# A GEGLU feed-forward kernel: first loads in a forced order, zero matmuls at the start, transposes of x by DMA, and halves outside quarters

## The chip, the cores and the metric

One core of one Trainium2 chip. The metric is device time in microseconds (us) of the whole program. The span is the time from the first to the last instruction in the profiled run; it is 1.7 to 2.0 us shorter than the time of that run.

## The reference

```python
B, S, D, F = 1, 2048, 1024, 3584          # bf16
def reference(x, w_gate, w_up, w_down):
    return (_gelu(x @ w_gate) * (x @ w_up)) @ w_down
```

## The kernel before

x is worked in two blocks of 1024 rows, each in two halves of 512 (`sh`). A block has a first phase (g = gate matmuls, u = up matmuls, then GELU on ACT and a product on DVE into hT) and a second phase (o = down matmuls). The weights of the first phase come in seven groups (`fg`) of 1 MB each for gate and up; each group has four quarters (`fi`) of 128 columns. The matmuls need x transposed. The tensor engine (PE) does that, in chunks (`sc`) of 128 rows, and DVE copies each chunk out of PSUM.

```python
w_pool = ...tile_pool(name="wstream", bufs=3)
xnat_pool = ...tile_pool(name="xnat", bufs=3)      # room for three x chunks
def load_xT_chunk(blk, sc):
    x_nat = xnat_pool.tile([P, D], bf16, name="x_nat")
    nc.sync.dma_start(out=x_nat[:], in_=x2[row0:row0 + P, :])
    for dc in range(DC):
        nc.tensor.transpose(pT[:, dc, :], x_nat[:, dc * P:(dc + 1) * P], ident[:])
    nc.vector.tensor_copy(out=xT_t[:, :, off:off + P], in_=pT[:])

for sc in range(SCB):                               # eight chunks first
    load_xT_chunk(0, sc)
for blk in range(NBLK):
    for fg in range(NFG):
        # 1 MB of gate, 1 MB of up, in block 0 also 1 MB of down, all on nc.sync
        for fi in range(FG):
            for sh in range(NSH):                   # quarter outer, half inner
                # 8 g matmuls, 8 u matmuls, gelu (ACT), product (DVE) -> hT
    for sc in range(SCB):
        # 2 x 28 o matmuls, copies (ACT), store (nc.scalar)
        if blk + 1 < NBLK:
            load_xT_chunk(blk + 1, sc)              # next block's x, on PE
```

## Time and profile before

| | before |
|---|---|
| time, median of 4 runs | 608.31 us (606.58 to 608.51) |
| span of the profiled run | 606.7 us |
| PE busy | 98%, 2816 matmuls and transposes |
| DVE, ACT busy | 14%, 14% |
| DMA | 74 GB/s of HBM traffic over the span |

PE is busy nearly throughout, so its busy share cannot tell where time is to be had. The readings that can are the chain that ended last, which names what the end of the program waited for, step by step, and the timeline of the first 25 us.

### The profile page before, as it was taken

The page shows a single profiled execution, that of the slowest core. Times are in us where ns is not written, and L with a number is a line of the kernel's source. Part 1 is how long each engine was busy: PE and PEld are TensorE (multiplying, and loading weights), DVE is VectorE, ACT ScalarE, POOL GpSimd, SP SyncE. Part 2 cuts the span into 40 slices and gives each one's busy share as a digit, 9 for nine tenths or more (in the row PEclk, how much of TensorE's full clock was granted, in tenths as well). Part 3 has the DMA queues.
Part 4 walks back from the last instruction along what each step waited for, and adds up shares of the span by engine and source line. Part 5 has one row for each costly group of instructions (what it writes and reads, how often), then busy time and mean ns, then how long its engine had stood idle before and what let it go on. Part 6 is the DMA issues. An engine that isn't in the chain of part 4 may idle for free.

```text
span 606.7 us, 6223 instructions
## 1 busy us (share of the span) xinstructions
PE 591.7 (98%) x2816; PEld 272.2 (45%) x2816; DVE 87.9 (14%) x128; ACT 86.9 (14%) x145; POOL 0.7 (0%) x6
## 2 busy tenths in 40 slices
PE   3999999999999999999999999999999999999997
PEld 2444444444444444444444444444444444444443
DVE  1221211212112100000001212112121120000000
ACT  0111111111111100101011111111111111101010
POOL 0000000000000000000000000000000000000000
PEclk9999999999999999999999999999999999999999
DMA  8997032140404041011000404041300000000000
GB/s 295 351 323 260 24 115 90 50 138 1 139 0 139 0 156 54 35 36 35 36 18 0 139 0 139 0 140 34 106 1 0 1 0 1 17 36 17 18 18 35
DMA packets 37451, 45.49 MB, mean 75 GB/s; under 512 B 1072, under 2 KB 29744, under 8 KB 37424
## 3 DMA queue, kind: packets, MB, share of 16 engines
q1 hardware_dynamic: 35120, 40.90, 20.8%
q10 hardware_dynamic: 2304, 4.20, 1.8%
q8 instruction: 22, 0.36, 0.2%
q14 instruction: 5, 0.04, 0.0%
HBM read 40.89 MB, written 4.19 MB: 74 GB/s over the span
## 4 chain that ended last, share of the span: by engine, by line
PE 97%; DMA 2%; DVE 0%; issue 0%; ACT 0%
PE g_ps L109 32%; PE u_ps L114 32%; PE o_ps L131 32%; DMA x_nat<-in_x_dram 2%; PE pT L79 1%; DVE xT L81 0%; DVE hT L120 0%; ACT o_sb L136 0%
## 5 line engine op out<-in xcount | busy, mean ns | idle before, releaser
L109 PE MATMUL g_ps<-xT,wg 128*128 128x512 bf16 x896 | 212.9, 381 | 0.6 <-DVE xT L81 0.6
L114 PE MATMUL u_ps<-xT,wu 128*128 128x512 bf16 x896 | 211.8, 379 | 0.0
L131 PE MATMUL o_ps<-wd,hT 128*128 128x512 bf16 x896 | 195.0, 379 | 0.0
L109 PEld LDWEIGHTS <-wg 128*128 128x128 bf16 x896 | 88.0, 98 | 107.0 <-issue 2.5
L114 PEld LDWEIGHTS <-wu 128*128 128x128 bf16 x896 | 87.7, 98 | 105.6
L131 PEld LDWEIGHTS <-hT 128*128 128x128 bf16 x896 | 87.3, 98 | 104.0 <-DVE hT L120 0.2
L120 DVE TENSOR_TENSOR hT<-hT,u_ps 128x512 bf16<-128x512 bf16 x112 | 77.1, 688 | 308.0 <-PE u_ps L114 308.0
L119 ACT ACTIVATE hT<-g_ps 128x512 bf16<-128x512 f32 x112 | 66.9, 597 | 335.2 <-PE g_ps L109 335.2
L136 ACT CAST o_sb<-o_ps 128x512 bf16<-128x512 f32 x32 | 18.8, 586 | 180.7 <-PE o_ps L131 180.7
L81 DVE COPY xT<-pT 128x1024 bf16<-128x1024 bf16 x16 | 11.0, 691 | 111.2 <-PE pT L79 111.2
L79 PE MATMUL pT<-ident,x_nat 128*128 128x128 bf16 x128 | 11.5, 248 | 10.7 <-DMA x_nat<-in_x_dram 10.6
L79 PEld LDWEIGHTS <-x_nat 128*128 128x128 bf16 x128 | 9.8, 112 | 13.6 <-DMA x_nat<-in_x_dram 11.1
L119 ACT ACT_TABLE_LOAD x1 | 1.3, 1283 | 0.7 <-PEq L154 0.7
masks.py:199 POOL TENSOR_SCALAR_AFFINE_SELECT ident<-ident 128x128 bf16<-128x128 bf16 x1 | 0.3, 294 | 0.1
masks.py:197 POOL MEMSET ident<- 128x128 bf16 x1 | 0.2, 205 | 0.3 <-POOLq L154 0.3
L154 POOL MEMSET const-uint8-127<- 128x1 uint8 x1 | 0.1, 103 | 0.0
L154 POOL MEMSET const-bfloat16-1.0<- 128x1 bf16 x1 | 0.1, 102 | 0.0
L154 POOL MEMSET const-float32-0.0<- 128x1 f32 x1 | 0.1, 99 | 0.2 <-issue 0.2
L154 POOL MEMSET const-float32-1.0<- 128x1 f32 x1 | 0.1, 99 | 0.0
## 6 DMA issues: line engine op xcount, KB each, us to landing
wg<-in_w_gate_dram SPq DMA_DIRECT2D x14, 1024.0 KB, 5.2
wu<-in_w_up_dram SPq DMA_DIRECT2D x14, 1024.0 KB, 7.7
wd<-in_w_down_dram SPq DMA_DIRECT2D x7, 1024.0 KB, 12.3
x_nat<-in_x_dram SPq DMA_DIRECT2D x16, 256.0 KB, 3.4
out_dram<-o_sb ACTq DMA_DIRECT2D x16, 256.0 KB, 2.0
```

What stands on the lines that cost most here:

```text
L79: nc.tensor.transpose(pT[:, dc, :], x_nat[:, dc * P:(dc + 1) * P], ident[:])
L81: nc.vector.tensor_copy(out=xT_t[:, :, off:off + P], in_=pT[:])
L109: nc.tensor.matmul(g_ps[:], lhsT=wg_t[:, dc, fi * P:(fi + 1) * P], rhs=xT_t[:, dc, :], start=(dc == 0), stop=(dc == DC - 1),)
L114: nc.tensor.matmul(u_ps[:], lhsT=wu_t[:, dc, fi * P:(fi + 1) * P], rhs=xT_t[:, dc, :], start=(dc == 0), stop=(dc == DC - 1),)
L119: nc.scalar.activation(h_t[:], g_ps[:], ACT.Gelu_apprx_tanh)
L120: nc.vector.tensor_tensor(out=h_t[:], in0=h_t[:], in1=u_ps[:], op=ALU.mult)
L131: nc.tensor.matmul(o_ps[:], lhsT=hT[(fc, sh)][:, off:off + P], rhs=wd_tiles[fc // FG][:, fc % FG, dh * DH:(dh + 1) * DH], start=(fc == 0), ...
L136: nc.scalar.copy(out=o_sb[:, dh * DH:(dh + 1) * DH], in_=o_ps[:])
L154: nc = _bacc.Bacc("TRN2", target_bir_lowering=False, num_devices=1)
```

## The change

It is meant to shorten everything that is not one of the 2688 large matmuls. It sends the first half of x and the first weights off at once on two hardware queues, in a forced order. It runs eight matmuls of zeros while PE would wait. It transposes only the first half of x on PE and leaves the other three halves to DMA transposes. It reads the first weight group in quarters, so that the first one is there early, and puts the halves outside the quarters in every group, so that the second half of x is wanted later. The order on PE is fixed by hand. Besides, the down weights are loaded one group later, the streamed weights have two buffers rather than three, and the output tiles share eight buffers with x. The cut below is shortened; `...` marks what is left out.

```diff
+N_WARM = 8; IO_BUFS = 8; W_BUFS = 2; FORCE_DMA_ORDER = True
-    w_pool = ...(name="wstream", bufs=3); xnat_pool = ...bufs=3; o_pool = ...bufs=2
+    w_pool = ...(name="wstream", bufs=W_BUFS); io_pool = ...(name="io", bufs=IO_BUFS)
+    zt = const_pool.tile([P, WN], bf16, name="zt")
+    nc.vector.memset(zt[:], 0.0)
+    for i in range(N_WARM):
+        nc.tensor.matmul(warm_ps[:, :WN], lhsT=zt[:, 0:P], rhs=zt[:, :], start=True, stop=True)
+    ctx.enter_context(tc.manual_schedule(engines={mybir.EngineType.PE}))
+    def load_xT_half_dma(blk, sh, dma_eng):
+        dma_eng.dma_start_transpose(out=xT_t[:, :, :], in_=x2[row0:row0 + SH, :])
-    for sc in range(SCB):
-        load_xT_chunk(0, sc)
+    for sc in range(SCH):      # x chunks 0, 2 on sync, 1, 3 on scalar
+        load_x_nat(0, sc, nc.sync if sc % 2 == 0 else nc.scalar, ...)
+    for fi in range(FG):       # quarters: rows of 256 B
+        stamp(nc.sync.dma_start(out=wg0_t[:, :, fi * P:(fi + 1) * P], ...), "sp")
+        stamp(nc.scalar.dma_start(out=wu0_t[:, :, fi * P:(fi + 1) * P], ...), "act")
+    for sh in range(1, NSH):
+        load_xT_half_dma(0, sh, nc.sync)
+    for sc in range(SCH):
+        transpose_x_chunk(0, sc)
 ...
+            # block 0, from fg 2 on: one DMA transpose of a half of block 1 per group
-            for fi in range(FG):
-                for sh in range(NSH):
+            for sh in range(NSH):
+                for fi in range(FG):
+                    phase1_group(blk, fg * FG + fi, sh, wg_t, wu_t, fi, hT)
 ...
-            if blk + 1 < NBLK:
-                load_xT_chunk(blk + 1, sc)
```

More of the change, by code (lines that the diff above doesn't have):

```diff
@@ L10 @@
 ALU = mybir.AluOpType
+N_WARM = 8
+IO_BUFS = 8
+W_BUFS = 2
+FORCE_DMA_ORDER = True
 @with_exitstack
@@ L54 @@
     hT_pool = ctx.enter_context(tc.tile_pool(name="hT", bufs=FC * NSH))
-    w_pool = ctx.enter_context(tc.tile_pool(name="wstream", bufs=3))
-    xnat_pool = ctx.enter_context(tc.tile_pool(name="xnat", bufs=3))
-    o_pool = ctx.enter_context(tc.tile_pool(name="osb", bufs=2))
+    w_pool = ctx.enter_context(tc.tile_pool(name="wstream", bufs=W_BUFS))
+    io_pool = ctx.enter_context(tc.tile_pool(name="io", bufs=IO_BUFS))
     ps_g = ctx.enter_context(tc.tile_pool(name="ps_g", bufs=2, space=bass.MemoryType.PSUM))
@@ L61, with stamp, get_xT @@
     ps_t = ctx.enter_context(tc.tile_pool(name="ps_t", bufs=2, space=bass.MemoryType.PSUM))
+    if N_WARM > 0:
+        WN = min(SH, DH)
+        zt = const_pool.tile([P, WN], bf16, name="zt")
+        nc.vector.memset(zt[:], 0.0)
+        warm_ps = ps_o.tile([P, DH], f32, name="o_ps")
+        for i in range(N_WARM):
+            nc.tensor.matmul(warm_ps[:, :WN], lhsT=zt[:, 0:P], rhs=zt[:, :], start=True, stop=True)
     ident = const_pool.tile([P, P], bf16, name="ident")
     make_identity(nc, ident[:])
+    def stamp(inst, tok):
+        if FORCE_DMA_ORDER and tok is not None:
+            tc.stamp_issue_order_token(inst.ins, tok)
+    ctx.enter_context(tc.manual_schedule(engines={mybir.EngineType.PE}))
     xT_tiles = {}
-    def load_xT_chunk(blk, sc):
-        sh = sc // SCH
+    def get_xT(blk, sh):
         key = (blk, sh)
@@ L72, in load_xT_chunk, with load_x_nat, transpose_x_chunk @@
             xT_tiles[key] = xT_pool.tile([P, DC, SH], bf16, name="xT")
-        xT_t = xT_tiles[key]
+        return xT_tiles[key]
+    x_nat_tiles = {}
+    def load_x_nat(blk, sc, dma_eng, tok=None):
         row0 = blk * SBLK + sc * P
-        x_nat = xnat_pool.tile([P, D], bf16, name="x_nat")
-        nc.sync.dma_start(out=x_nat[:], in_=x2[row0:row0 + P, :])
+        x_nat = io_pool.tile([P, D], bf16, name="io")
+        stamp(dma_eng.dma_start(out=x_nat[:], in_=x2[row0:row0 + P, :]), tok)
+        x_nat_tiles[(blk, sc)] = x_nat
+    def transpose_x_chunk(blk, sc):
+        sh = sc // SCH
+        xT_t = get_xT(blk, sh)
+        x_nat = x_nat_tiles.pop((blk, sc))
         pT = ps_t.tile([P, DC, P], bf16, name="pT")
@@ L81, in load_xT_chunk, with load_wd, phase1_group @@
         nc.vector.tensor_copy(out=xT_t[:, :, off:off + P], in_=pT[:])
+    def load_xT_half_dma(blk, sh, dma_eng):
+        xT_t = get_xT(blk, sh)
+        row0 = blk * SBLK + sh * SH
+        dma_eng.dma_start_transpose(out=xT_t[:, :, :], in_=x2[row0:row0 + SH, :])
     wd_tiles = []
-    def load_wd(fg):
+    def load_wd(fg, dma_eng):
         t = wd_pool.tile([P, FG, D], bf16, name="wd")
-        nc.sync.dma_start(out=t[:], in_=wd_v[:, fg * FG:(fg + 1) * FG, :])
+        dma_eng.dma_start(out=t[:], in_=wd_v[:, fg * FG:(fg + 1) * FG, :])
         wd_tiles.append(t)
-    for sc in range(SCB):
-        load_xT_chunk(0, sc)
+    def phase1_group(blk, fc, sh, wg_t, wu_t, fi, hT):
+        xT_t = xT_tiles[(blk, sh)]
+        g_ps = ps_g.tile([P, SH], f32, name="g_ps")
+        u_ps = ps_u.tile([P, SH], f32, name="u_ps")
+        for dc in range(DC):
+            nc.tensor.matmul(
+                g_ps[:], lhsT=wg_t[:, dc, fi * P:(fi + 1) * P], rhs=xT_t[:, dc, :],
+                start=(dc == 0), stop=(dc == DC - 1),
+            )
+        for dc in range(DC):
+            nc.tensor.matmul(
+                u_ps[:], lhsT=wu_t[:, dc, fi * P:(fi + 1) * P], rhs=xT_t[:, dc, :],
+                start=(dc == 0), stop=(dc == DC - 1),
+            )
+        h_t = hT_pool.tile([P, SH], bf16, name="hT")
+        nc.scalar.activation(h_t[:], g_ps[:], ACT.Gelu_apprx_tanh)
+        nc.vector.tensor_tensor(out=h_t[:], in0=h_t[:], in1=u_ps[:], op=ALU.mult)
+        hT[(fc, sh)] = h_t
+    wg0_t = w_pool.tile([P, DC, FG * P], bf16, name="wg")
+    wu0_t = w_pool.tile([P, DC, FG * P], bf16, name="wu")
+    for sc in range(SCH):
+        load_x_nat(0, sc, nc.sync if sc % 2 == 0 else nc.scalar, "sp" if sc % 2 == 0 else "act")
+    for fi in range(FG):
+        stamp(nc.sync.dma_start(out=wg0_t[:, :, fi * P:(fi + 1) * P],
+                                in_=wg_v[:, :, fi * P:(fi + 1) * P]), "sp")
+        stamp(nc.scalar.dma_start(out=wu0_t[:, :, fi * P:(fi + 1) * P],
+                                  in_=wu_v[:, :, fi * P:(fi + 1) * P]), "act")
+    for sh in range(1, NSH):
+        load_xT_half_dma(0, sh, nc.sync)
+    for sc in range(SCH):
+        transpose_x_chunk(0, sc)
+    pending_xT = [(b_, sh_) for b_ in range(1, NBLK) for sh_ in range(NSH)]
     for blk in range(NBLK):
@@ L95 @@
         for fg in range(NFG):
-            wg_t = w_pool.tile([P, DC, FG * P], bf16, name="wg")
-            nc.sync.dma_start(out=wg_t[:], in_=wg_v[:, :, fg * FG * P:(fg + 1) * FG * P])
-            wu_t = w_pool.tile([P, DC, FG * P], bf16, name="wu")
-            nc.sync.dma_start(out=wu_t[:], in_=wu_v[:, :, fg * FG * P:(fg + 1) * FG * P])
-            if blk == 0:
-                load_wd(fg)
-            for fi in range(FG):
-                fc = fg * FG + fi
-                for sh in range(NSH):
-                    xT_t = xT_tiles[(blk, sh)]
-                    g_ps = ps_g.tile([P, SH], f32, name="g_ps")
-                    u_ps = ps_u.tile([P, SH], f32, name="u_ps")
-                    for dc in range(DC):
-                        nc.tensor.matmul(
-                            g_ps[:], lhsT=wg_t[:, dc, fi * P:(fi + 1) * P], rhs=xT_t[:, dc, :],
-                            start=(dc == 0), stop=(dc == DC - 1),
-                        )
-                    for dc in range(DC):
-                        nc.tensor.matmul(
-                            u_ps[:], lhsT=wu_t[:, dc, fi * P:(fi + 1) * P], rhs=xT_t[:, dc, :],
-                            start=(dc == 0), stop=(dc == DC - 1),
-                        )
-                    h_t = hT_pool.tile([P, SH], bf16, name="hT")
-                    nc.scalar.activation(h_t[:], g_ps[:], ACT.Gelu_apprx_tanh)
-                    nc.vector.tensor_tensor(out=h_t[:], in0=h_t[:], in1=u_ps[:], op=ALU.mult)
-                    hT[(fc, sh)] = h_t
@@ new lines @@
+            c0 = fg * FG * P
+            if blk == 0 and fg == 0:
+                wg_t, wu_t = wg0_t, wu0_t
+            else:
+                wg_t = w_pool.tile([P, DC, FG * P], bf16, name="wg")
+                wu_t = w_pool.tile([P, DC, FG * P], bf16, name="wu")
+                nc.sync.dma_start(out=wg_t[:], in_=wg_v[:, :, c0:c0 + FG * P])
+                nc.sync.dma_start(out=wu_t[:], in_=wu_v[:, :, c0:c0 + FG * P])
+            if blk == 0:
+                if fg >= 1:
+                    load_wd(fg - 1, nc.sync)
+                if fg == NFG - 1:
+                    load_wd(fg, nc.sync)
@@ L123 @@
+            if blk == 0 and pending_xT and (fg >= 2 or fg == NFG - 1):
+                n_issue = 1 if fg < NFG - 1 else len(pending_xT)
+                for _ in range(n_issue):
+                    b_, sh_ = pending_xT.pop(0)
+                    load_xT_half_dma(b_, sh_, nc.sync)
+            for sh in range(NSH):
+                for fi in range(FG):
+                    phase1_group(blk, fg * FG + fi, sh, wg_t, wu_t, fi, hT)
         for sc in range(SCB):
@@ L126 @@
             row0 = blk * SBLK + sc * P
-            o_sb = o_pool.tile([P, D], bf16, name="o_sb")
+            o_sb = io_pool.tile([P, D], bf16, name="io")
             for dh in range(NDH):
```

## The prediction

> **What bounds the kernel now.** I read the page's busy shares first, then the chain that ended last, because busy time of pipelined matmuls does not say how close to its floor the engine runs.
>
> ```profile
> span 606.7 us, 6223 instructions
> PE 591.7 (98%) x2816; PEld 272.2 (45%) x2816; DVE 87.9 (14%) x128; ACT 86.9 (14%) x145; POOL 0.7 (0%) x6
> PE g_ps L109 32%; PE u_ps L114 32%; PE o_ps L131 32%; DMA x_nat<-in_x_dram 2%; PE pT L79 1%; DVE xT L81 0%; DVE hT L120 0%; ACT o_sb L136 0%
> L79 PE MATMUL pT<-ident,x_nat 128*128 128x128 bf16 x128 | 11.5, 248 | 10.7 <-DMA x_nat<-in_x_dram 10.6
> ```
>
> The tensor engine is the chain: 96% is the three matmul groups, 2% waiting for x, 1% transposes of x. DVE and ACT are 14% busy and release nothing late. So only the 2%, the 1% and the pace of the matmuls are to be had. The chain in order of time gives the pace and the head (columns: start, length, what):
>
> ```profile
> 0.74 2.56 DMA x_nat<-in_x_dram
> 4.41 9.02 DMA x_nat<-in_x_dram
> 13.47 1.89 PE pT L79 x16
> 15.36 3.06 PE g_ps L109 x8
> 22.96 1.89 PE g_ps L109 x8
> 506.27 96.71 PE o_ps L131 x448
> ```
>
> The last row is the pace: 96.71 / 448 = 0.2159 us for each 128x512 matmul. There are 3 x 896 = 2688, so the unavoidable part is 580.3 us. The span is 606.7, so 26.4 us are something else. The timeline tells what (start, length, engine, line, what):
>
> ```profile
> 19.77 0.61 PE L79 MATMUL pT<-ident,x_nat 128*128 128x128 bf16 x8
> 20.43 1.33 PE L79 MATMUL pT<-ident,x_nat 128*128 128x128 bf16 x16
> 22.96 1.89 PE L109 MATMUL g_ps<-xT,wg 128*128 128x512 bf16 x8 [0.59 <-DVE xT L81]
> 224.54 0.61 PE L79 MATMUL pT<-ident,x_nat 128*128 128x128 bf16 x8
> 603.00 0.59 ACT L136 CAST o_sb<-o_ps 128x512 bf16<-128x512 f32 x1 [5.46 <-PE o_ps L131]
> ```
>
> The account of the 26.4 us:
> - 15.4 us until the first g matmul at 15.36. The fourth x chunk has a buffer only at 4.41 and then queues behind 2 MB of gate and up weights, hence the 9.02 us in the chain.
> - 1.3 us: the first eight g matmuls take 3.06 us, where eight at pace take 1.73.
> - 2.4 us: from 18.42 to 22.96 (4.54 us) the engine does eight u and, reordered forward, two o matmuls, ten at pace = 2.16 us; the rest, 2.4, is transposes of the second half of x and a wait on their copy.
> - 3.5 us: eight chunks of the next block are transposed between o groups. A pair of o groups with its transposes repeats every 12.53 us; 56 matmuls at pace are 12.09; 8 x 0.44 = 3.5.
> - 3.7 us after the last matmul (602.98 to 606.7): last copy and last store.
> They sum to 26.3, so nothing large is hidden elsewhere.
>
> **What the Trainium skill says.** (1) "TensorE: Matmul & The Clock Gate", Part 1: the array starts at half clock, is released after about 3.4 us of sustained activity, and falls back after an idle window of about that length; warm matmuls of 512 columns follow each other at N/2.4 + 2.5 ns, 215.8. The trace agrees: 215.9 ns, and a slow first eight. (2) "DMA: Bandwidth & Descriptors", Specifications: transfers want rows of at least 512 B, below it there is a read-modify-write. The trace has only rows of 1 and 2 KB in bulk (364 to 376 GB/s between 7 and 12 us in the windows view), so what 256 B rows do is not shown. (3) The same page, Latency and other measured facts: a crossbar DMA transpose moved 261 GB/s in one kernel. (4) "VectorE: DVE Perf Modes", The three transpose paths: one 128x128 block by that path takes 1309 ns. No run here shows either yet, and they are far apart: 1 MB at 261 GB/s is 4.0 us, 32 blocks end to end would be 42 us.
>
> **The change part by part.**
>
> *Early loads.* Four x chunks go out at once, two on each hardware queue, ahead of any weight, with four buffers of their own. In the windows view the core had moved 0.83 MB by 5 us and 1.1 MB by 6:
>
> ```profile
> 2.00:3.00 1.00, 0.00 (x0) 0.00 (x0) 0.00 (x0) 0.02 (x1) 0.00 (x0) 1.00 1.01 318
> 3.00:4.00 1.00, 0.65 (x7) 0.66 (x8) 0.00 (x0) 0.00 (x0) 0.00 (x0) 1.00 0.73 225
> 10.00:11.00 1.00, 0.00 (x0) 0.00 (x0) 0.00 (x0) 0.00 (x0) 0.00 (x0) 1.00 1.08 368
> ```
>
> (last column GB/s, the one before it the share of the DMA engines; the dip at 3 to 5 us is beside slow issue on one queue). With two queues I put the 1 MB of x at about 5.2 us. Then the first quarter of gate and up, 0.52 MB in 256 B rows: I take half of 368 GB/s as an estimate from point (2), 2.9 us, plus 0.5 for landing: 8.6. The transposes of the fourth chunk (0.95 us) and its copy (0.69) fit before that. First g matmul at about 9.0 instead of 15.36: 6.4 us gained.
>
> *Warm-up.* Eight zero matmuls of 512 columns at half clock, 8 x 0.43 = 3.4 us, stand in front of the transposes and fit in the wait for x, which in the trace ends at 3.3. They cost about nothing and should let the first g group run at pace: 1.3 us gained.
>
> *Second half of x and all of the second block by DMA transpose.* Of 128 PE transposes 96 go, and 12 copies on DVE. On the path: the 2.4 us around 20 us and the 3.5 us between the o groups: 5.9 us gained.
>
> *Order and buffers.* Manual order of the tensor engine ends the pulling forward of o matmuls; nothing else in it moves. With two weight buffers rather than three, a load may start when the group before last is done, and has one group's time, 8 x 8 x 2 x 0.2159 = 27.6 us, to arrive; the page has 5.2 and 7.7 us to landing. Hidden. The tail is untouched.
>
> *Supply.* This is the new cost. With the halves outer, the first 4 groups read only the first half of x, but all four quarters of gate and up: one pair per 3.45 us, at 2.9 us supply. The pairs come just ahead. The last pair has left the queue at 5.2 + 4 x 2.9 = 16.8; then the transpose of the second half, behind them on the same queue: 4.0 us at 261 GB/s plus some 1.5 for landing, 22.3. It is wanted at 9.0 + 4 x 3.45 = 22.8. There is no slack, so any slower rate than either assumption is paid in full: at half the transpose rate 4 us. I book 2.0 us.
>
> Sum: -6.4 - 1.3 - 5.9 + 2.0 = -11.6; 608.3 - 11.6 = 596.7; I say 596.5. As a cross-check: 9.0 + 580.3 + 3.7 = 593.0 of span, and runs are 1.6 us longer than the profiled span (608.31 against 606.7): 594.6 with no stall.
>
> **The rivals.**
>
> *The transpose DMA takes the place of the wait removed.* If the crossbar moves about 75 GB/s, the second half lands near 32 us, the engine idles 9 us at the end of the first four groups, goes cold, and the time is 604 to 606. For it: the figure of 1309 ns a block, and no trace of this path. Against: someone laid out one such transfer per later weight group, where it is hidden anyway, and put only one at the critical place. The second block's transfers have over 150 us; they cannot matter.
>
> *Narrow rows starve the start.* If 256 B rows cost as much time as 1 KB rows (47 ns per packet and engine: 16 x 1.08 x 1024 B / 368 GB/s), a pair takes 6 us, the four pairs end at 29, and everything after is late by 8 to 13 us: 603 to 608, no gain. For it: the pace per packet in the trace is only known where bytes bind. Against: 1 KB and 2 KB rows move at nearly equal rates, so a fixed cost per row is not seen at 1 KB.
>
> *All fits.* Both assumptions are a little pessimistic, t0 is 8.5 and no stall: 594. For it: queues issue at 0.4 us each and two share the start.
>
> **Range and chances.** The gain without stalls is 13.6 us, 2.2%, so the 2% line (596.1) leaves only 1.5 us for stalls. Stalls under 1.5 us I hold for 0.46, between that and 26 us for 0.51, above 26 for 0.03, which would need the transpose DMA to take 30 us. The range 592.5 to 604.0 leaves out the full form of the first two rivals.
>
> **What would show it.** Right: first g matmul near 9 us and its eight taking 1.7 to 1.9 us; 32 PE transposes; no transposes among the o groups, which then run at 0.2159 without a break; last matmul to end still 3.7 us. Wrong: gaps before g or u groups put down to the weight DMAs (narrow rows), or one gap before the fifth pair put down to xT by DMA (slow transpose); or a wait for weights in later groups (two buffers too few).

## The result, and the profile after

| | before | after |
|---|---|---|
| median | 608.23 us (13 runs, 606.58 to 608.54) | 594.08 us (8 runs, 593.78 to 596.69) |
| span of the profiled run | 606.7 us | 592.2 us |
| first g matmul starts | 15.36 us | 8.35 us |
| PE transposes | 128 | 32 |

The ratio is 0.9777, with a 95% interval of 0.9765 to 0.9789: faster by 2.2%. Ratios are the mean time of one kernel's runs over that of the other's of the same rounds, so they are not quite the ratio of the medians quoted. The predicted time was 596.5 with a range of 592.5 to 604.0. The measured time lies in the range, 2.4 us below the point. Of the three chances, "within 2%" had 0.51 and "faster by over 2%" 0.46; the second came, so the class held for slightly more likely did not.

The page of the changed kernel, busy shares and chain by line:

```profile
PE 586.4 (99%) x2728; PEld 266.4 (45%) x2728; DVE 79.9 (13%) x117; ACT 87.0 (15%) x145; POOL 0.7 (0%) x6
PE g_ps L126 33%; PE o_ps L189 33%; PE u_ps L131 33%; PE o_ps L73 1%; DVE xT L107 0%; PE pT L105 0%; ACT io L194 0%; DVE zt L70 0%
```

No DMA is left in the chain: before, x had 2% of it. What remains is 33% for each kind of matmul and 1% for the zero matmuls (L73). Rows of the timeline of PE, its weight loads (PEld), DVE and SyncE's queue (SPq) in the first 25 us (start, length, engine, line, what, idle before and what ended it):

```profile
1.19 3.59 PE L73 MATMUL o_ps<-zt 128*128 128x512 bf16 x8 [1.19 <-DVE zt L70]
4.57 1.45 PE L105 MATMUL pT<-ident,io 128*128 128x128 bf16 x16
5.62 2.68 DVE L107 COPY xT<-pT 128x1024 bf16<-128x1024 bf16 x4 [4.49 <-PE pT L105]
7.82 9.06 SPq L112 DMA_TRANSPOSE xT<-in_x_dram  x1
7.84 0.10 PEld L126 LDWEIGHTS <-wg 128*128 128x128 bf16 x1 [0.45 <-DMA wg<-in_w_gate_dram]
8.35 1.89 PE L126 MATMUL g_ps<-xT,wg 128*128 128x512 bf16 x8 [0.78 <-DVE xT L107]
...
22.16 1.89 PE L126 MATMUL g_ps<-xT,wg 128*128 128x512 bf16 x8
```

The g row at 8.35 is the new start. The first gate quarter has landed at 7.84 and what is waited for last is the fourth copy on DVE, from a row of four that ends at 8.30. The next u group begins 1.72 us later, which is eight times the pace of 0.2159: no slow first group. The g row at 22.16 is the first that reads the second half of x, and it has no wait in brackets. By the view of the DMA transpose's source, that transfer took 12.7 us from its issue at 7.82, so it landed at 20.5, 1.7 us before it was wanted. Most of that time it stood behind the weight quarters. From 16 to 18 us the queue moved nothing but its rows of 256 B, at 290 GB/s (columns: us, busy time by engine, granted clock, DMA share, GB/s):

```profile
16.00:18.00 2.00, 2.00 (x11) 0.88 (x9) 0.21 (x1) 0.60 (x1) 0.00 (x0) 1.00 1.28 290
```

From 8.35 to the end of the last matmul nothing stops PE: in the changed trace the second phase of the first block takes from 201.73 to 298.43, 96.70 us for 448 matmuls, where the kernel before had 8 x 12.53 = 100.2. The chain in order of time has them as one piece (start, length, what):

```profile
201.90 96.69 PE o_ps L189 x448
```

So the 14.5 us between the two spans are:

| where | before | after | gain |
|---|---|---|---|
| start of the first g group | 15.36 | 8.35 | 7.0 |
| first g group, over the pace | 1.3 | 0 | 1.3 |
| transposes and their wait near 20 us | 2.4 | 0 | 2.4 |
| transposes among the o groups | 3.5 | 0 | 3.5 |
| after the last matmul | 3.7 | 3.5 | 0.2 |

They add up to 14.4.

### The profile page after: what moved, and what is told of

It reads as the page before. It is cut to its first block, busy times and chain, and to the rows that moved or that the text cites. A ratio compares the mean times of both kernels' runs of the same rounds, so it can differ in the third digit from the quotient of the medians.

```text
span 592.2 us, 6019 instructions
## 1 busy us (share of the span) xinstructions
PE 586.4 (99%) x2728; PEld 266.4 (45%) x2728; DVE 79.9 (13%) x117; ACT 87.0 (15%) x145; POOL 0.7 (0%) x6
## 4 chain that ended last, share of the span: by engine, by line
PE 99%; DVE 0%; ACT 0%; issue 0%
PE g_ps L126 33%; PE o_ps L189 33%; PE u_ps L131 33%; PE o_ps L73 1%; DVE xT L107 0%; PE pT L105 0%; ACT io L194 0%; DVE zt L70 0%
## 5 line engine op out<-in xcount | busy, mean ns | idle before, releaser
L194 ACT CAST io<-o_ps 128x512 bf16<-128x512 f32 x32 | 18.8, 586 | 178.1 <-PE o_ps L189 178.1
L73 PE MATMUL o_ps<-zt 128*128 128x512 bf16 x8 | 3.6, 631 | 1.2 <-DVE zt L70 1.2
L107 DVE COPY xT<-pT 128x1024 bf16<-128x1024 bf16 x4 | 2.6, 686 | 4.6 <-PE pT L105 4.5
L105 PE MATMUL pT<-ident,io 128*128 128x128 bf16 x32 | 2.7, 241 | 0.3 <-DVE xT L107 0.3
L105 PEld LDWEIGHTS <-io 128*128 128x128 bf16 x32 | 2.4, 110 | 1.2 <-issue 0.6
L73 PEld LDWEIGHTS <-zt 128*128 128x128 bf16 x8 | 1.0, 140 | 2.8 <-issue 1.7
```

The lines of the kernel that those rows point to most:

```text
L73: nc.tensor.matmul(warm_ps[:, :WN], lhsT=zt[:, 0:P], rhs=zt[:, :], start=True, stop=True)
L194: nc.scalar.copy(out=o_sb[:, dh * DH:(dh + 1) * DH], in_=o_ps[:])
```

## The experiments

My theory after the result: five places add up, and what makes the gain come in full is that two new supplies (weight quarters, DMA transpose) are both just in time. Its rivals: one part alone (x earlier, or the forced order) makes the gain and the rest is idle; or the zero matmuls do nothing; or the DMA transpose is in time under any order. Each edit below is to the changed kernel unless said otherwise. The extra time of an edit is given against the change's median of 594.08 or its span of 592.2. The experiments ran in later rounds on chips 14, 6 and 1; the kernel before ran beside them, with medians of 608.23, 608.39 and 607.93 us, so differences of a few tenths of a us are not read.

### nowarm, nowarm2, nowarm3: without the zero matmuls

```diff
-N_WARM = 8
+N_WARM = 0
```

> The change without its eight zero matmuls. My theory: the array is still at half clock when the first g group starts, so that group takes about 3.1 us rather than 1.9 as in the kernel before; against that the transposes can begin some 0.4 us earlier, since in the changed kernel they wait for the zero matmuls as long as for x. Net: 1.0 us longer than the change, about 595.1. Rival: the 32 transposes warm the array themselves; then the first g group takes 1.9 us and the run is equal to the change or 0.4 us faster.

Measured: 595.1 us in the median of four runs, but these are two pairs: 593.99 and 594.18, 596.03 and 596.41. The traced one was a quick one, with a first g group at pace at 8.58. So the median met the theory while the trace met the rival.

> The kernel without zero matmuls once more, for its trace alone: its runs fell into 594.0 to 594.2 and 596.0 to 596.4, and only a quick one was traced, in which the first g group ran at pace. My theory now: the slow ones are those in which the array is still at half clock in the first g groups (1.7 us each); if this look is a slow one, its first g group takes over 3 us and starts near 8.6 as well. Rival: the slow ones wait for data, so the first g group starts 2 us later and takes 1.9.

> The same kernel a third time, to have a second chance of a slow run in the trace; the expectations are those of the look before it.

The first of these looks took 594.18 us, the second 596.67: a quick and a slow one. First PE's timeline in nowarm2, the quick one:

```profile
4.09 3.68 PE L105 MATMUL pT<-ident,io 128*128 128x128 bf16 x32 [4.09 <-DMA io<-in_x_dram]
8.56 1.89 PE L126 MATMUL g_ps<-xT,wg 128*128 128x512 bf16 x8 [0.78 <-DVE xT L107]
```

Then in nowarm3, the slow one:

```profile
4.46 3.68 PE L105 MATMUL pT<-ident,io 128*128 128x128 bf16 x32 [4.46 <-DMA io<-in_x_dram]
8.93 3.57 PE L126 MATMUL g_ps<-xT,wg 128*128 128x512 bf16 x8 [0.78 <-DVE xT L107]
12.29 2.39 PE L131 MATMUL u_ps<-xT,wu 128*128 128x512 bf16 x8
```

The slow run starts 0.4 us later, and its first g and u group take 3.36 us and 2.23 us to the start of the next rather than 1.73: 2.1 us over the pace together. With the 0.4 that is the 2.5 us between the two spans (594.9 and 592.4). So without the zero matmuls the array can still be at half clock when the first group starts. That is shown in one slow run; the two other slow ones of six (596.03 and 596.41) were not traced, and that they have the same cause is likely and not shown. With the zero matmuls, one of the change's eight runs (596.69) is slow. In the quick runs that were traced the 32 transposes alone had warmed the array. Both theory and rival held, in different runs. What the zero matmuls are worth in the mean is not settled: the means differ by 0.8 us, but the ratios to the kernel before, 0.9781 (0.9761 to 0.9802) and 0.9777 for the change, do not tell them apart, and the recorded verdict is unclear. They mostly take away spread.

### fiouter: quarter outer, half inner, as before

```diff
-            for sh in range(NSH):
-                for fi in range(FG):
+            for fi in range(FG):
+                for sh in range(NSH):
```

> The change with the old loop order, quarter outer and half inner. My theory: the halves-outer order is what hides the DMA transpose. The second half of x lands at 20.5 us in the changed kernel and is wanted at 11.8 us here, so the tensor engine stalls 8.7 us once, goes cold for another 1.3 us, and the run is about 604. Rival: the order only helps the weights, and the transpose would be in time anyway: 594.

Measured: 602.92 us (602.59 to 603.17), 8.8 over the change. PE's timeline in fiouter:

```profile
9.88 1.89 PE L131 MATMUL u_ps<-xT,wu 128*128 128x512 bf16 x7
18.84 3.47 PE L126 MATMUL g_ps<-xT,wg 128*128 128x512 bf16 x8 [7.07 <-DMA xT<-in_x_dram]
22.14 1.89 PE L131 MATMUL u_ps<-xT,wu 128*128 128x512 bf16 x8
```

One stall of 7.07 us, ended by the DMA transpose, and behind it a g group at half clock (3.30 us from 18.84 to 22.14). The transfer landed at 18.8 here and not at 20.5, which is why the stall is shorter than expected. The order of the loops is what hides the transpose: swapped back, most of the gain is gone.

### wide: first weights in rows of 1 KB

```diff
-    for fi in range(FG):
-        ... dma_start(out=wg0_t[:, :, fi * P:(fi + 1) * P], ...)   # and wu0_t
+    ... dma_start(out=wg0_t[:], in_=wg_v[:, :, 0:FG * P])          # and wu0_t
```

> The change with the first gate and up weights in one transfer each with rows of 1 KB, not four quarters with rows of 256 B. My theory: the first g group now has to wait for all of gate, which shares the engines with up; 1 MB of x and 2 MB of weights at about 350 GB/s land near 11.5 us, so the first g matmul comes about 3 us later than 8.35 and the run is about 597. Rival: the narrow rows (218 GB/s in the changed trace) lose what the quarters gain, and the run is within 0.5 us of the change.

Measured: 600.99 us (600.1 to 601.28), 6.9 over the change; the profiled run has 5.9 more span. PE's timeline in wide:

```profile
11.35 3.60 PE L126 MATMUL g_ps<-xT,wg 128*128 128x512 bf16 x8 [3.48 <-DMA wg<-in_w_gate_dram]
...
17.59 1.89 PE L126 MATMUL g_ps<-xT,wg 128*128 128x512 bf16 x8
```

The start is at 11.35, 3.0 later, as the theory said. What it left out is the clock: PE idled 3.48 us, and the next 16 matmuls took 6.24 us (17.59 - 11.35) instead of 3.45. 3.0 + 2.8 are the 5.9, within rounding. So the narrow rows pay although they are slow. The windows view of the changed kernel has them by themselves at 9 to 10 us (last columns: granted clock, DMA share, GB/s):

```profile
9.00:10.00 1.00, 1.00 (x6) 0.48 (x5) 0.00 (x0) 1.00 (x1) 0.00 (x0) 1.00 1.35 218
```

218 GB/s against 364 to 376 for rows of 1 KB in the kernel before: 0.59 of it.

### blk1pe: second block of x on PE again

```diff
-                    load_xT_half_dma(b_, sh_, nc.sync)      # block 1, with its loop
+            if blk + 1 < NBLK:                              # after each output tile
+                load_x_nat(blk + 1, sc, nc.sync)
+                transpose_x_chunk(blk + 1, sc)
```

> The change with the second block of x transposed on the tensor engine between the o groups again, as in the kernel before. My theory: 64 transposes cost 8 x 0.44 = 3.5 us of the engine, and nothing else moves: 597.6. Rival: the DMA transposes cost something too (disturbed weight loads), so that undoing them costs less than 3.5 us.

Measured: 597.62 us (597.49 to 598.06), 3.5 over the change, the number of the theory. PE's timeline in blk1pe:

```profile
202.04 12.25 PE L183 MATMUL o_ps<-wd,hT 128*128 128x512 bf16 x55
214.13 0.61 PE L105 MATMUL pT<-ident,io 128*128 128x128 bf16 x8
214.57 12.25 PE L183 MATMUL o_ps<-wd,hT 128*128 128x512 bf16 x54
```

A row of transposes stands between o groups that start at 202.04 and 214.57: 12.53 us, as in the kernel before.

### half1pe: second half of the first block on PE

```diff
-        load_xT_half_dma(0, sh, nc.sync)
+        load_x_nat(0, sc, nc.sync)                          # four chunks
+                if blk == 0 and fg == 0 and sh == 1:
+                    for sc in range(SCH, SCB):
+                        transpose_x_chunk(0, sc)
```

> The change with the second half of the first block loaded plainly and transposed on the tensor engine between its first four and next four groups, in place of the DMA transpose. My theory: the engine pays 32 transposes (1.8 us) and waits for the four copies behind them (4 x 0.69, the first starting 0.5 us in): 3.3 us between 22.2 and 25.5, so 597.4. Rival: the DMA transpose is worth no more than its 1.8 us of matmuls, because the copies overlap: 595.9.

Measured: 598.21 us (598.05 to 598.74), 4.1 over the change. PE's timeline in half1pe:

```profile
22.22 1.06 PE L105 MATMUL pT<-ident,io 128*128 128x128 bf16 x16
23.83 1.21 PE L105 MATMUL pT<-ident,io 128*128 128x128 bf16 x16 [0.55 <-DVE xT L107]
25.82 1.90 PE L126 MATMUL g_ps<-xT,wg 128*128 128x512 bf16 x8 [0.79 <-DVE xT L107]
```

From 22.22 to 25.82 are 3.6 us: the transposes and two waits on DVE's copies (0.55 and 0.79 of them visible in the brackets). The theory had 3.3, the rival 1.8. The profiled run also has half a microsecond more after the last matmul, which I do not explain. The DMA transpose of this half is worth more than the transposes themselves, because PE does not wait for copies.

### noorder: first transfers in the scheduler's own order

```diff
-FORCE_DMA_ORDER = True
+FORCE_DMA_ORDER = False
```

> The change without the forced order of its first transfers. The built program then has x chunk, gate quarter, x chunk, gate quarters on one queue, and up quarter, x chunk, up quarter, x chunk, up quarters on the other. My theory: the last x chunk lands behind up to 1 MB of narrow rows, near 9 us rather than 5.5 to 6; transposes and copy put the first g matmul near 10.6 rather than 8.35: 2.2 us, and up to 1.5 more if the array goes cold meanwhile: 596.3 to 597.8. Rival: the same bytes have to come anyway, so the first g group waits no longer: 594.

Measured: 600.17 us (599.05 to 600.52), 6.1 over the change and outside both expectations. PE's timeline in noorder:

```profile
10.16 1.04 PE L105 MATMUL pT<-ident,io 128*128 128x128 bf16 x8 [1.44 <-DMA io<-in_x_dram]
11.98 3.57 PE L126 MATMUL g_ps<-xT,wg 128*128 128x512 bf16 x8 [0.78 <-DVE xT L107]
...
18.24 1.89 PE L126 MATMUL g_ps<-xT,wg 128*128 128x512 bf16 x8
```

The last x chunk landed at 10.1 rather than near 9, the first g group came at 11.98, 3.6 later than in the change, and its 16 matmuls with u ran cold: 18.24 - 11.98 = 6.26 us, 2.8 over the pace. The mechanism was right, the size short by the second cold group and one more microsecond of landing.

### earlyx: the kernel before with five x buffers

```diff
-    xnat_pool = ...tile_pool(name="xnat", bufs=3)
+    xnat_pool = ...tile_pool(name="xnat", bufs=5)
```

> The kernel before with one number changed: five buffers for x chunks rather than three, so that the first half of x is not queued behind the weights. My theory: this alone takes back most of the head. Gate lands near 9 us and the first g matmul comes then instead of at 15.4; but the last three chunks still land behind up, near 13.5 us, and their transposes stand in the middle of the first g group, so that group ends near 15 us. From there 2680 matmuls at 0.2159, 3.5 us of later transposes and 3.7 of tail: a span near 601 and a time near 602.5, 6 us under the kernel before. Rival: it is the order of the weights that sets the start, and x earlier only moves the wait: within 1 us of 608.

Measured: 605.85 us (605.18 to 606.65) against 608.39 of the kernel before in the same rounds, ratio 0.9961 (0.9947 to 0.9975): 2.5 us, not 6. PE's timeline in earlyx:

```profile
10.34 1.25 PE L109 MATMUL g_ps<-xT,wg 128*128 128x512 bf16 x5 [1.65 <-DMA wg<-in_w_gate_dram]
14.00 1.03 PE L79 MATMUL pT<-ident,x_nat 128*128 128x128 bf16 x8 [2.41 <-DMA x_nat<-in_x_dram]
...
20.01 1.89 PE L109 MATMUL g_ps<-xT,wg 128*128 128x512 bf16 x8
```

The first g matmul is indeed 5 us earlier. But gate lands at 10.3 and not 9, the group is broken off for the last three chunks, which land behind up, and its last matmuls and the u group run slow: 16 matmuls are done by 20.01. The kernel before had 18 done by 22.96. 2.95 less the two matmuls (0.43) is the measured 2.5. Here the rival was nearer: x alone mostly moves the wait. This is not the change's early load by itself, since the last three chunks still stand before the first group here. That the parts of the change need each other also follows from the losses when one is undone: 8.8, 6.9, 3.5, 4.1 and 6.1 us (fiouter, wide, blk1pe, half1pe, noorder) add up to 29.4, twice the 14.2 that was gained.

### best and best2: a shorter start

The first try cut each copy out of PSUM in two and stored the last tile in pieces:

```diff
-        nc.vector.tensor_copy(out=xT_t[:, :, off:off + P], in_=pT[:])
+        hd = DC // 2
+        nc.vector.tensor_copy(out=xT_t[:, :hd, off:off + P], in_=pT[:, :hd, :])
+        nc.vector.tensor_copy(out=xT_t[:, hd:, off:off + P], in_=pT[:, hd:, :])
+        # ... and the last output tile: stored in three pieces, its last 512 columns copied by DVE and ACT
```

> The change with two edits that follow from its trace: each copy of a transposed chunk is cut in two, so that the first g matmuls start when the first half of the last copy is done (bound then by gate landing at 7.84 rather than by the copy ending at 8.3), and the last output tile is stored in three pieces, the last 512 columns copied by two engines. My theory: 0.35 us at the start, 0.4 at the end; 593.3. Rival: the fixed cost of two more copies per chunk on DVE eats the gain at the start, and the last store is bound by its fixed time: within 0.3 us of the change.

Measured: 593.83 us (593.19 to 596.54), 0.25 under the change and so not told apart from it, as the rival said. Its profiled run happened to be its slow one (596.54), and shows what such a run is:

```profile
9.38 3.52 PE L128 MATMUL g_ps<-xT,wg 128*128 128x512 bf16 x8 [1.53 <-DMA wg<-in_w_gate_dram]
12.74 1.89 PE L133 MATMUL u_ps<-xT,wu 128*128 128x512 bf16 x7
```

The first gate quarter landed at 9.3 rather than 7.84, the array fell to half clock meanwhile, and the group took 3.36 us. Against the change that is 1.0 us of start and 1.6 of clock, the 2.6 us between the two spans (594.8 and 592.2). The end was not shortened: the span ends 3.5 us after the last matmul, as in the change. The change's own slow run (596.69) has the same size; it was not traced, so that it has the same cause is likely and not shown. The second try therefore also gives gate the DMA engines to itself:

```diff
-N_WARM = 8
+N_WARM = 7
+        # chunks 2, 3: pT = ps_u.tile(...), not ps_t; chunk 1: nc.scalar.copy
-        stamp(nc.scalar.dma_start(out=wu0_t[...], ...), "act")
+        stamp(nc.sync.dma_start(out=wu0_t[...], ...), "sp")
```

> The change with a shorter start: seven zero matmuls rather than eight, the third and fourth chunk transposed into other PSUM buffers so that they need not wait for copies, the second chunk copied by ACT, and the up quarters on the same queue as the gate quarters, so that the first gate quarter does not share the DMA engines with up. My theory: the start is bound by the four copies in a row on DVE (5.62 to 8.30) and by gate landing at 7.84; with both shorter the first g matmul comes near 7.6 and the time is 593.3, and the spread upwards of single runs (596.5 and more when the first quarter is late and the array goes cold) becomes rarer. Rival: something else sets the start, the landing of the last x chunk above all; then it stays at 8.2 and the time at 594.

Measured: 593.31 us (593.22 to 593.68, five runs), ratio to the kernel before 0.9758 (0.9745 to 0.9772). PE's timeline in best2:

```profile
5.49 1.07 PE L108 MATMUL u_ps<-ident,io 128*128 128x128 bf16 x16
7.58 1.89 PE L132 MATMUL g_ps<-xT,wg 128*128 128x512 bf16 x8 [1.03 <-DVE xT L113]
```

The start moved from 8.35 to 7.58, where it was expected, and the span from 592.2 to 591.5. It beats the kernel before clearly. Against the change it is 0.8 us in the medians and 0.7 in the spans, while the two ratio intervals overlap; the trace's start is the better evidence. The first gate quarter landed at 6.9 (5.2 us from its issue at 1.67) rather than 7.84, and the last copy on DVE ended at 7.43 rather than 8.30; the four edits were made together, so what each is worth is not shown. That none of its five runs was slow fits the expectation, but one in eight before is too few to call the spread cured.

One part needed no run: with the hand-made order on PE taken out, the program that is built has the same PE instructions in the same order (compared one by one, with buffer numbers left out), so this part of the change does nothing here.

## Why the prediction was right

- **The bound and the account of 26.4 us.** Right. The pace of 0.2159 us holds in the changed trace (448 matmuls in 96.70 us), and the entries of the account shrank one by one as the table of the result shows.
- **Early loads.** Right in mechanism; predicted start 9.0, measured 8.35. The term mis-sized is the weight pair: half of the wide rows' rate was assumed, 2.9 us for 0.52 MB; the measured 218 GB/s make it 2.4. What the prediction had wrong in the path is the copy: it counted the fourth alone, 0.69 us, and let gate's landing end the wait. In the trace DVE's four copies stand in a row, 5.62 to 8.30, and end it, 0.46 us after gate. Shortening the copies and gate's landing together moved the start (best2).
- **Warm-up.** The 1.3 us came. That the zero matmuls bring it was only half right: without them two of three traced runs warmed up on transposes alone (nowarm, nowarm2). Nor do they quite fit in the wait for x: they start at 1.19 and end at 4.78, while without them the transposes start at 4.1.
- **DMA transposes.** Right: 3.5 us among the o groups (blk1pe, 3.5 when undone) and 2.4 near 20 us. The alternative by PE in the new order would have cost 3.6 (half1pe).
- **Order and buffers.** Right that two weight buffers suffice: PE waits for no weights after 7.84 us. The remark that manual order ends the pulling forward of o matmuls was wrong as to cause: the program is the same without it.
- **Supply.** This is the step that failed in size. It booked 2.0 us for a shortfall, and the shortfall was 0: the transfer landed at 20.5 against an estimate of 22.3, and was wanted at 22.2. The mis-sized term is again the weight pairs: the last was to leave the queue at 16.8, and the up queue moved its last rows before 15. With the 0.65 us of the start this is the difference between 596.7 and 594.1.
- **The rivals.** "All fits" is the one that came. The slow transpose did not: 12.7 us from issue, much of it behind the weight quarters, and 8.8 in best2. Its 290 GB/s are above the 261 assumed and far above the 75 of the rival; 42 us for the 32 blocks end to end is ruled out. Starved narrow rows did not: 218 GB/s and not a quarter of the wide rate. But fiouter shows how near the first rival lies: with the old loop order the same transfer stops PE for 7 us.
- **What the account left out.** Runs in which PE waited 1.5 to 7 us before or in the first groups also paid 1.6 to 2.8 us of half clock (best, noorder, wide, fiouter). The rival with the long stall named a cold array, but the prediction had no such term for smaller stalls.
- **Small slips.** The 47 ns of the second rival are 48 by its own figures, the 1.5 us left for stalls are 1.4, and the 1.6 us between time and span are 1.8 when both are taken from the same run (608.51 and 606.7); nothing hangs on them.

## What to carry to other kernels

When PE is at its pace for 95% of the time, list what is left of the span entry by entry and read each from the timeline; the entries can be predicted and then checked one by one. A start is a supply problem: send first what the first group needs and no more, even in rows that move slower per byte, and order the groups so that each piece is wanted just after it can land. A slow transfer is free where it is early enough and costs its full lateness, and then the cold array behind it, where it is not.

## What the Trainium skill lacked or had wrong

- "TensorE: Matmul & The Clock Gate", Part 4, says that the full clock does not engage for transposes, as they do not count as busy in the same way. The runs do not bear this out in general: in nowarm2 there were 32 transposes and no matmul before the first g group, and it ran at pace (1.73 us for eight); in nowarm3 it did not (3.36). So transposes can warm the array, and whether they have by a given moment varies from run to run. In best the clock fell at 9.3 us although the 3.4 us before held 1.6 us of transposes; whether these did not count or were too few is open.
- Its Part 1 gives about 3.4 us of sustained activity for the release, varying by 0.5 us either way in one place and from 6 to 14 slow matmuls in another. The runs show the wider spread: from the first g matmul after the stall to the release it was 3.2 us in fiouter, 3.3 in best and 5.7 in wide and noorder. The window of 3.4 us that runs freely, in the same Part, fits this: by the granted-clock column, read from the shares of the slices, the clock fell at 9.3, 15.2, 10.2, 11.9 and 7.5 us and came back at 12.7, 22.1, 17.0, 18.7 and 17.7 (best, fiouter, wide, earlyx, noorder), which is 3.4, 6.8, 6.8, 6.8 and 10.2 us later, each time a whole number of windows. In these five runs it came back at the end of the first window in which PE was at work from within 0.2 us of its start; that this is the rule is an inference from them.
- "DMA: Bandwidth & Descriptors", Specifications, says that rows under 512 B lose line rate, without a factor. Its section "Why small descriptors are slow (HBM only)" has 27% of overhead for descriptors of 256 B. Rows of 256 B lost more here: 218 GB/s, 0.59 of what rows of 1 KB did.
- Part 1 also warns that the records of clock changes have been unreliable, but no page says this: the granted-clock column of the windows view reads 1.00 in the first microseconds of the changed kernel, although the zero matmuls there follow each other at 0.43 us, half pace. It shows a later fall (0.50 in noorder from 8 to 17 us), but not the cold start.
